# A fused attention and two-mixture kernel: last logits among the next output sums, sums read before low parts, first gathered transposes over two units

## Chip, cores and metric

The kernel runs on one core of a Trainium2 chip. The metric is device microseconds (us) of one execution; a profiled execution also has a span, from its first to its last recorded instruction. Engines are named as in the profile: PE is TensorE (PEld its weight loads), DVE is VectorE, ACT is ScalarE, POOL is GpSimd, SP is SyncE, whose queue issues most DMAs.

## The reference, cut to what matters

Attention with a bucket mask runs first; its output `x` (1536 tokens of 512) goes through a dense layer pair, and the result through a mixture of eight experts, each token by the one expert with the largest logit.

```python
def _moe_ref(x, w_in, w_out, s, b):            # first mixture: 512 -> 2048 -> 512
    h = x @ w_in
    r = np.maximum(h, 0.0)
    g = s * (r * r) + b
    return (g @ w_out).astype(np.float32)

def _moe2_ref(x, modality_id, w_gate, modality_bias, w1, w2):   # second: 8 experts, 512 -> 1024 -> 512
    logits = x @ w_gate + modality_bias[modality_id]
    e_idx = np.argmax(logits, axis=1)
    ...
    for e in range(E):
        mask = e_idx == e
        h = np.maximum(x[mask] @ w1[e], 0.0)
        out[mask] = gate_w[mask, None] * (h @ w2[e])
```

## The kernel before

All products are made from high and low halves: a 32-bit value is split by ACT into a rounded high part and by DVE into the rest, and each product is three matmuls (high x high, high x low, low x high).

**Units.** After attention, PE works through a list of units written out in `program`. The first mixture has three token groups of 512 (`g` = 0, 1, 2) and 16 hidden chunks of 128 (`fc`). A unit `(0, g, fc)` multiplies one hidden chunk into the four output slices `Y0` to `Y3` (`y1`, line 863, 12 matmuls of 512 columns). The last unit of a group ends with `yout` (line 883): DVE adds the saved partial sums `sv` to the four slices and writes the output sums `yt`. The second mixture works on blocks of up to 408 tokens of one expert. A unit `(1, s, fc)` multiplies hidden chunk `fc` (of 8) of block `s` into the same four slices (`sb_o`, line 1181, 12 matmuls of 408 columns). Its last unit ends with `sb_out`, where ACT and DVE copy the slices to `ot` (lines 1191 and 1189).

**Lead.** Each unit first issues the hidden product of the unit two places later (`h1`, line 820, or `sb_h`, line 1161; a product `H` is 12 matmuls). What ACT and DVE do to that product is a post: `r` in the first mixture (lines 826 and 827) and `hh` and `hl` in the second (lines 1168 and 1169), which share their two buffers each with `gh` and `gl` of the first (lines 834 and 835). In the last two units of the first mixture and in all of the second, the post is issued late, after the unit's output sums:

```python
            (self.sb_o if u[0] else self.y1)(u[1], u[2])
            self.flush()
            if late:
                post[0]()
            if u[2] == (7 if u[0] else 15):
                (self.sb_out if u[0] else self.yout)(u[1])
```

**Side jobs.** `at(kind, a, fc, ...)` hangs jobs on a unit. They are taken in their order, one after each quarter of the hidden product if marked with `n > 0` (and as long as the first in the list is so marked), and the rest after the four output slices, as many at a time as makes them fit into four places. The table `MT` says on which `fc` a job stands.

**The jobs around the change.** The tokens of groups 0 and 1 are routed while group 2 is computed. `sb_gather(0)` fetches the rows of block 0 from DRAM with four gathers of POOL (line 1134), of 128, 128, 128 and 24 rows, on unit `(0, 2, 10)`. `sb_xt(0, d)` for `d` = 0 to 3 transposes them, four 128x128 transposes of PE each (`mxt` from `xg`, line 1148), into one of two PSUM banks that all small jobs share in turn; ACT copies the high part `xh` and DVE the low part `xl` (lines 1149 and 1150). All four stand on unit `(0, 2, 13)`, beside the last weight split (lines 1067 and 1068).
On unit `(1, 0, 0)` stand, for the tokens of group 2, four `ylog` (each four matmuls of `yt` by the gate's 8 columns, `ml`, line 891, and an add into the logits `L`, line 893), marked to go between the quarters of the hidden product. Then come `rest_a` (the choice of an expert, lines 917 to 970, and one activation) and two `yrow` (four transposes `mr`, line 900, a copy by ACT, and a store to DRAM by SP's queue, line 904). Unit `(1, 0, 1)` has `rest_b` (rank matmuls, lines 979 to 984, then a chain of DVE up to `pos`, lines 988 to 1026) and six one-hots `M` (line 1088). Unit `(1, 0, 2)` has two more `yrow`, `rest_c` (the expert numbers for SP's loads), the first `sb_pick` (`mid`, line 1100) and six more one-hots.

Of the kernel before, what the change touches and what calls it, by code (L numbers as in the profile page):

```python
# [610 lines left out]
NG = 3  # L611
# [4 lines left out]
class Moe:  # L616
# [618 lines left out]
    def program(self, open_route, end_attn, close_attn, end1):  # L1235
        side = {}
        self.lo_engine = self.nc.vector

        def at(kind, a, fc, *fns, n=0):

            side.setdefault((kind, a, fc), []).extend(([x, None, n > 0], n) for x in fns)

        units = [(0, g, fc) for fs in (range(FA), range(FA, 16)) for g in range(NG) for fc in fs]
        n1 = len(units)
        units += [(1, s, fc) for s in range(NSB) for fc in range(8)]

        def ids(s, n, kind, a, fc, step):
            i = units.index((kind, a, fc))
            for lo in range(0, n, step):
                hi = min(n, lo + step)  # L1250
                at(*units[i], *(lambda tb=tb: self.sb_onehot(s, tb) for tb in range(lo, hi)))
                i += 1
                at(*units[i], lambda lo=lo, hi=hi: self.sb_pick(s, lo, hi), n=(hi - lo) // 2 + 1)
            at(*units[i], lambda: self.sb_ids(s), lambda: self.sb_gather(s))


        at(0, 0, MT["xt"], end_attn)
        at(0, 0, max(MT["xt"], self.led - LEAD), close_attn)
        for i in range(34 - self.wi):
            at(*units[(0, 0, 1, 2)[i] if i < 4 else i * 3 // 4], self.w_next)  # L1260
        for g in range(NG - 1):
            for t in range(4):
                at(0, g + 1, FA + (t + 1, t // 2)[g], lambda g=g, t=t: self.ylog(g, t), n=1)
                at(0, g + 1, FA + t + 1 - g, lambda g=g, t=t: self.yrow(g, t))
        at(0, 1, 14, open_route)
        at(0, 1, 15, lambda: self.setup_route(self.rt))
        g = NG - 1
        at(0, g, MT["fa"], self.first_a)
        at(0, g, MT["fb"], self.first_b)
        at(0, g, MT["fc"], self.first_c)  # L1270
        W0 = self.sb_weights(0, lambda: self.e0[0:1, 0:1])
        for i in range(8):
            at(0, g, MT["w0"] + i // 2, W0[i][0])
            at(0, g, MT["w0"] + (i + 1) // 2 + 1, W0[i][1])
        ids(0, TA, 0, g, MT["i0"], 4)
        for d in range(4):
            at(0, g, MT["x0"], lambda d=d: self.sb_xt(0, d))

        for t in range(4):
            at(1, 0, 0, lambda t=t: self.ylog(NG - 1, t), n=1)  # L1280
        at(1, 0, 0, self.rest_a)
        for t in range(2):
            at(1, 0, MT["ya"], lambda t=t: self.yrow(NG - 1, t))
        at(1, 0, MT["rb"], self.rest_b)
        for t in range(2, 4):
            at(1, 0, MT["yb"], lambda t=t: self.yrow(NG - 1, t))
        at(1, 0, MT["rc"], self.rest_c)
        for s in range(NSB):
            n = s + 1
            if s:  # L1290
                for c in range(NC):
                    at(1, s, c // 2, lambda s=s, c=c: self.sb_store(s - 1, c))
            if n == NSB:
                continue
            ids(n, 12, 1, s - 1 if s else 0, MT["iN"] if s else MT["i1"], MT["sn"] if s else MT["s1"])
            for d in range(4):
                at(1, s, MT["xn"] + d // 2 if s else MT["x1"], lambda n=n, d=d: self.sb_xt(n, d))
            W = self.sb_weights(n, lambda n=n: self.ei[0:1, n:n + 1])
            for i in range(8):
                a = i if s else MT["w1"] + i // 2 + (i == 7)  # L1300
                at(1, s, a, W[i][0])
                if a == 7:
                    at(1, n, 0, W[i][1])
                else:
                    at(1, s, a + 1, W[i][1])

        def lead(u):
            return (self.sb_h if u[0] else self.h1)(u[1], u[2])

        while self.led < LEAD:  # L1310
            self.lead1()
        self.lead2()
        self.lead3(LEAD)
        none = lambda: None
        for i, u in enumerate(units):
            mine = side.pop(u, [])
            self.jobs.extend(x[0] for x in mine)
            if i + LEAD < self.led:
                post = none, self.posts[i + LEAD][0]
            else:  # L1320
                post = lead(units[i + LEAD]) if i + LEAD < len(units) else (none, none)
            late = i + LEAD >= n1
            if not late:
                post[0]()
            self.rate = -(-sum(max(n, 1) for x, n in mine if x in self.jobs) // 4)
            (self.sb_o if u[0] else self.y1)(u[1], u[2])
            self.flush()
            if late:
                post[0]()
            if u[2] == (7 if u[0] else 15):  # L1330
                (self.sb_out if u[0] else self.yout)(u[1])
            elif not u[0] and u[2] == FA - 1:
                self.ysave(u[1])
            if i == n1 - 1:
                end1()
            post[1]()
        for c in range(NC):
            self.sb_store(NSB - 1, c)


LEAD = 2
NST = 3
MT = dict(xt=0, fa=6, fb=7, fc=8, w0=8, i0=8, x0=13, ya=0, yb=2, rb=1, rc=2, i1=1, s1=6, x1=5, xn=3, w1=3, iN=5, sn=6)

FA = 4
NM = 6
# [128 lines left out]
```

## Time and profile before

| what | us |
|---|---|
| median of the three runs shown | 750.51 |
| all three | 757.81, 749.63, 750.51 |
| profiled execution | 752.84 |
| its span | 751.0 |
| PE busy | 698.9 (93%) |
| DVE, ACT, POOL busy | 429.1, 364.7, 248.6 |
| mean granted clock of PE in the profile | 0.966 of full speed |

A timeline row is: start, length, engine, line, operation, what is written from what, shape, count; in brackets the idle time of the engine before it and what ended that. Matmuls overlap, so the step from one start to the next says what one costs. The granted clock is 1.00 at 2.4 GHz and 0.50 at 1.2 GHz.

### The profile page before, as it was taken

What the parts mean: (1) busy time and instruction counts of PE and PEld (TensorE: products, weight loads), DVE (VectorE), ACT (ScalarE), POOL (GpSimd) and SP (SyncE); (2) the same over time, 40 slices, a digit from 0 to 9 for tenths busy, and PEclk for the clock granted to TensorE, in tenths of its full rate; (3) what the DMA queues carried; (4) which work ended last, traced back from release to release, by engine and by line L of the source; (5) the groups of instructions that cost most, each with busy time, mean ns of one, the idle gap of its engine ahead of it and who ended that gap; (6) DMA issues with size and microseconds to landing.
All of it is one profiled execution on the core that took longest, in us unless ns stands there. A gap on an engine that the chain in (4) does not pass through costs nothing.

```text
span 751.0 us, 12828 instructions
## 1 busy us (share of the span) xinstructions
PE 698.9 (93%) x5037; PEld 613.4 (82%) x5037; DVE 429.1 (57%) x781; ACT 364.7 (49%) x562; POOL 248.6 (33%) x251
## 2 busy tenths in 40 slices
PE   6688899999999689999999999999998999999993
PEld 5587788988988677788888888888878989999993
DVE  5455667667667976988773322235653565645311
ACT  2565687877878755655542222222440254434412
POOL 8295777776878860000000000200200024030112
PEclk9699999999999889999999999999997999999998
DMA  6979435645470221534410010002420455435201
GB/s 150 216 173 217 87 72 111 138 108 112 108 183 2 86 85 61 154 123 121 131 57 0 1 43 14 1 29 87 139 72 1 139 160 201 141 109 161 69 17 43
DMA packets 53509, 73.64 MB, mean 98 GB/s; under 512 B 30456, under 2 KB 30968, under 8 KB 53440
## 3 DMA queue, kind: packets, MB, share of 16 engines
q1 hardware_dynamic: 50320, 63.49, 32.3%
q0 software_dynamic: 2960, 9.24, 3.9%
q8 instruction: 41, 0.67, 0.4%
q14 instruction: 28, 0.23, 0.1%
q10 hardware_dynamic: 160, 0.00, 0.0%
HBM read 46.37 MB, written 6.49 MB: 70 GB/s over the span
## 4 chain that ended last, share of the span: by engine, by line
PE 71%; ACT 8%; issue 7%; DVE 6%; POOL 4%; DMA 3%; SPq 0%; POOLq 0%; ACTq 0%; DVEq 0%
PE Y L863 17%; PE H L820 17%; PE H L1161 8%; PE Y L1181 7%; PE Sst L403 5%; PE av L424 5%; ACT e L405 3%; PE Smaxp L357 3%; POOL el L412 2%; PE Sbits L240 2%; PE ml L891 1%; ACT eh L411 1%; DVE v L716 1%; PE Strans L192 1%; PE SH L820 1%
## 5 line engine op out<-in xcount | busy, mean ns | idle before, releaser
L412 POOL TENSOR_TENSOR el<-e,eh 128x768 f16<-128x768 f32 x80 | 133.1, 1668 | 67.8 <-ACT eh L411 55.2
L863 PE MATMUL Y<-gh,W 128*128 128x512 f32 x384 | 131.5, 395 | 0.6 <-DVE sv L873 0.6
L359 DVE TENSOR_REDUCE mx<-Smaxp 128x1 f32<-128x768 f32 x96 | 90.5, 953 | 48.2 <-PE Smaxp L357 48.0
L405 ACT ACTIVATE e<-Sst 128x768 f32<-128x768 f32 x96 | 76.9, 802 | 45.8 <-PE Sst L403 43.5
L403 PE MATMUL Sst<-Q,K 128*128 128x384 f32 x384 | 94.3, 369 | 1.5 <-ACT e L405 1.3
L863 PEld LDWEIGHTS Y<-gh,W 128*128 128x128 f32 x384 | 72.1, 188 | 16.7 <-DVE sv L873 1.1
L1181 PE MATMUL Y<-hh,W 128*128 128x408 f32 x256 | 82.7, 364 | 0.0
L863 PE MATMUL Y<-gl,W 128*128 128x512 f32 x192 | 75.3, 392 | 0.0
L827 DVE SCALAR_TENSOR_TENSOR r<-r,sb 128x512 f32<-128x512 f32 x46 | 35.9, 781 | 68.6 <-ACT r L826 68.6
L403 PEld LDWEIGHTS Sst<-Q,K 128*128 128x128 f32 x384 | 66.3, 198 | 3.7 <-ACT e L405 1.5
L411 ACT ACTIVATE eh<-e 128x768 f16<-128x768 f32 x80 | 67.5, 844 | 2.5
L826 ACT ACTIVATE r<-H 128x512 f32<-128x512 f32 x44 | 26.3, 598 | 81.4 <-PE H L820 81.2
L801 POOL IOTA ev<- 128x96 f32 x1 | 0.3, 299 | 194.3 <-PE H L820 194.3
L357 PE MATMUL Smaxp<-K,Q 96*128 96x384 f32 x192 | 51.6, 359 | 13.3 <-ACT NM L392 4.6
L1134 POOL DMA_INDIRECT xg<-yd,ix x16 | 18.3, 1147 | 129.4 <-DVE nf L1120 69.0
L834 ACT ACTIVATE gh<-r,sb 128x512 fp32r<-128x512 f32 x46 | 33.0, 720 | 51.7 <-PE Y L863 49.8
L835 DVE SCALAR_TENSOR_TENSOR gl<-r,sb,gh 128x512 fp32r<-128x512 f32 x46 | 34.4, 749 | 37.1 <-ACT gh L834 37.1
L424 PE MATMUL av<-VX,eh 128*128 128x65 f16 x960 | 52.6, 197 | 2.0 <-ACT eh L411 2.0
L424 PEld LDWEIGHTS <-eh 128*128 128x128 f16 x960 | 40.2, 100 | 15.0 <-issue 12.1
L357 PEld LDWEIGHTS Smaxp<-K,Q 96*128 96x128 f32 x192 | 35.4, 198 | 18.9 <-ACT NM L392 6.6
L1068 DVE TENSOR_TENSOR W<-st,W 128x1024 fp32r<-128x1024 f32 x32 | 38.9, 1225 | 18.2 <-ACT W L1067 17.8
L1181 PEld LDWEIGHTS Y<-hh,W 128*128 128x128 f32 x256 | 48.9, 192 | 0.0
(321 smaller groups left out, 1485.4 us busy)
## 6 DMA issues: line engine op xcount, KB each, us to landing
st<-in_moe_w_dram SPq DMA_DIRECT2D x32, 512.0 KB
sw<-in_moe_w_in_dram SPq DMA_DIRECT2D x16, 512.0 KB
sw<-in_moe_w_out_dram SPq DMA_DIRECT2D x16, 512.0 KB
Q<-qh SPq DMA_DIRECT2D x32, 192.0 KB
K<-kh SPq DMA_DIRECT2D x32, 192.0 KB
nq<-in_q_dram SPq DMA_DIRECT2D x16, 192.0 KB
nk<-in_k_dram SPq DMA_DIRECT2D x16, 192.0 KB
Q<-ql SPq DMA_DIRECT2D x16, 192.0 KB
```

Source lines behind the costliest of these rows:

```text
L357: nc.tensor.matmul(out=ps[:, a, 0:HALF], lhsT=self.Q1[i][0:96, j * 128:j * 128 + 128], rhs=self.K1[i][0:96, a * HALF:a * HALF + HALF])
L359: nc.vector.tensor_reduce(out=self.mx[h][:, j:j + 1], in_=ps[:, :, 0:HALF], axis=AX.XY, op=ALU.max)
L403: nc.tensor.matmul(out=ps[:, a, 0:HALF], lhsT=K[:, c], rhs=Q[:, a * HALF:a * HALF + HALF], start=(n == 0), stop=(n == 1))
L405: nc.scalar.activation(out=h2(e), in_=ps[:, :, 0:HALF], func=ACTF.Exp, scale=0.125)
L411: nc.scalar.activation(out=eh, in_=e, func=ACTF.Copy)
L412: nc.gpsimd.tensor_tensor(out=el, in0=e, in1=eh, op=ALU.subtract)
L424: mm = lambda q, n, e, v, start=False, stop=False: nc.tensor.matmul(out=av[:, q, 0:n], lhsT=e, rhs=v, start=start, stop=stop, skip_group_c ...
L820: nc.tensor.matmul(out=ps, lhsT=w[:, k, fs], rhs=x[:, k], start=(n == 0), stop=(n == 11))
L863: nc.tensor.matmul(out=self.yp[d], lhsT=w[:, i, ds], rhs=x, start=(fc in (0, FA) and n == 0), stop=(fc in (FA - 1, 15) and n == 2))
L1068: nc.vector.tensor_tensor(out=lo[:, o], in0=d["st"], in1=f(hi[:, o]), op=ALU.subtract)
L1161: nc.tensor.matmul(out=ps, lhsT=w, rhs=xx[:, kd, 0:C], start=(n == 0), stop=(n == 11))
L1181: nc.tensor.matmul(out=self.yp[d][:, 0:C], lhsT=w, rhs=xx, start=(fc == 0 and n == 0), stop=(fc == 7 and n == 2))
```

## The change

Two things are moved; no instruction is added or taken away.

1. The late post is issued after `yout` and `sb_out`. The four `ylog` of the last group are no longer marked to go between the quarters of the hidden product of unit `(1, 0, 0)`: three of them stand after its output slices 0, 1 and 3, the fourth after the first quarter of the hidden product of unit `(1, 0, 1)`. `rest_a` and the first two `yrow` move to that unit's product as well, and four empty jobs keep places ahead of `rest_b`.
2. The transposes of the first gathered rows stand on units `(0, 2, 12)` and `(0, 2, 13)`, two each, with an empty job after each.

```diff
+        nop = lambda: None
...
         for d in range(4):
-            at(0, g, MT["x0"], lambda d=d: self.sb_xt(0, d))
-
-        for t in range(4):
-            at(1, 0, 0, lambda t=t: self.ylog(NG - 1, t), n=1)
-        at(1, 0, 0, self.rest_a)
+            at(0, g, MT["x0"] + d // 2, lambda d=d: self.sb_xt(0, d), nop)
+
+        yl = [lambda t=t: self.ylog(NG - 1, t) for t in range(4)]
+        at(1, 0, 0, yl[0], yl[1], nop, yl[2])
+        at(1, 0, 1, yl[3], self.rest_a, n=1)
         for t in range(2):
-            at(1, 0, MT["ya"], lambda t=t: self.yrow(NG - 1, t))
+            at(1, 0, 1, lambda t=t: self.yrow(NG - 1, t), n=1)
+        at(1, 0, 1, *[nop] * 4)
         at(1, 0, MT["rb"], self.rest_b)
...
             self.flush()
-            if late:
-                post[0]()
             if u[2] == (7 if u[0] else 15):
                 (self.sb_out if u[0] else self.yout)(u[1])
             elif not u[0] and u[2] == FA - 1:
                 self.ysave(u[1])
+            if late:
+                post[0]()
...
-MT = dict(xt=0, fa=6, fb=7, fc=8, w0=8, i0=8, x0=13, ya=0, yb=2, rb=1, rc=2, i1=1, s1=6, x1=5, xn=3, w1=3, iN=5, sn=6)
+MT = dict(xt=0, fa=6, fb=7, fc=8, w0=8, i0=8, x0=12, yb=2, rb=1, rc=2, i1=1, s1=6, x1=5, xn=3, w1=3, iN=5, sn=6)
```

On DVE, at the end of the first mixture, the queue reads as follows before and after (`H_4355` and `H_4356` are the two product banks, `Y_4357` to `Y_4360` the four slices, `mx` is the first step of the choice).

```order
-L1169 SCALAR_TENSOR_TENSOR hl<-H_4356,hh 128x408
 L883 TENSOR_TENSOR yt<-Y_4357,sv_4621 128x512
 L883 TENSOR_TENSOR yt<-Y_4358,sv_4621 128x512
 L883 TENSOR_TENSOR yt<-Y_4359,sv_4621 128x512
 L883 TENSOR_TENSOR yt<-Y_4360,sv_4621 128x512
-L893 TENSOR_TENSOR L<-ml,L 128x8 x4
-L917 TENSOR_REDUCE mx_6609<-L 128x4
-L919 TENSOR_TENSOR eq<-L,mx_6609 128x32
+L1169 SCALAR_TENSOR_TENSOR hl<-H_4356,hh 128x408
+L893 TENSOR_TENSOR L<-ml,L 128x8 x3
+L1169 SCALAR_TENSOR_TENSOR hl<-H_4355,hh 128x408
+L893 TENSOR_TENSOR L<-ml,L 128x8
```

The low part of chunk 1 goes behind the four output sums, and that of chunk 2 behind the first three logits, ahead of the choice.

On PE, at the start of the second mixture, before: the hidden product of chunk 2 with the logits between its quarters.

```order
L1161 MATMUL H_4355<-xh,W 128x408
L1161 MATMUL H_4355<-xl,W 128x408
L1161 MATMUL H_4355<-xh,W 128x408
L891 MATMUL ml<-wg,yt 128x8 x4
L1161 MATMUL H_4355<-xh,W 128x408
L1161 MATMUL H_4355<-xl,W 128x408
L1161 MATMUL H_4355<-xh,W 128x408
L891 MATMUL ml<-wg,yt 128x8 x4
```

The same place after it: the end of that product, and the first two output slices of unit `(1, 0, 0)`.

```order
L1161 MATMUL H_4355<-xl,W 128x408
L1161 MATMUL H_4355<-xh,W 128x408
L1181 MATMUL Y_4357<-hh,W 128x408
L1181 MATMUL Y_4357<-hl,W 128x408
L1181 MATMUL Y_4357<-hh,W 128x408
L891 MATMUL ml<-wg,yt 128x8 x4
L1181 MATMUL Y_4358<-hh,W 128x408
L1181 MATMUL Y_4358<-hl,W 128x408
L1181 MATMUL Y_4358<-hh,W 128x408
L891 MATMUL ml<-wg,yt 128x8 x4
```

The first logits now stand behind the whole product and one output slice.

On PE, in unit `(0, 2, 12)`, between the output slices 1, 2 and 3:

```order
 L863 MATMUL Y_4358<-gl,W 128x512
 L863 MATMUL Y_4358<-gh,W 128x512
+L1148 MATMUL mxt<-ident,xg 128x128 x4
 L863 MATMUL Y_4359<-gh,W 128x512
 L863 MATMUL Y_4359<-gl,W 128x512
 L863 MATMUL Y_4359<-gh,W 128x512
+L1148 MATMUL mxt<-ident,xg 128x128 x4
 L863 MATMUL Y_4360<-gh,W 128x512
 L863 MATMUL Y_4360<-gl,W 128x512
```

Two groups of transposes stand here now, one unit earlier than before.

## Rows read from the trace of the kernel before

**Rows 1.** The page, parts 1 and 2: busy time, and granted clock in 40 slices
```profile
PE 698.9 (93%) x5037; PEld 613.4 (82%) x5037; DVE 429.1 (57%) x781; ACT 364.7 (49%) x562; POOL 248.6 (33%) x251
...
PEclk9699999999999889999999999999997999999998
```

**Rows 2.** Stages of 1 us: busy (x instructions) of PE, PEld, DVE, ACT, POOL; clock, DMA
```profile
572.00:573.00 1.00, 1.00 (x9) 1.00 (x9) 0.17 (x1) 0.00 (x0) 0.00 (x0) 1.00 0.00 0
573.00:574.00 1.00, 1.00 (x6) 1.00 (x6) 0.17 (x1) 0.00 (x0) 0.00 (x0) 0.52 0.06 16
...
583.00:584.00 1.00, 1.00 (x8) 0.93 (x7) 0.00 (x0) 0.19 (x1) 0.00 (x0) 0.86 0.21 84
```

**Rows 3.** Timeline of the seam: start, length, engine, line, what, idle before
```profile
567.84 0.35 PE L1161 MATMUL H<-xh,W 128*128 128x408 f32 x1
568.21 0.34 PE L1161 MATMUL H<-xh,W 128*128 128x408 f32 x1
...
568.58 0.58 DVE L1169 SCALAR_TENSOR_TENSOR hl<-H,hh 128x408 fp32r<-128x408 f32 x1 [4.32 <-ACT hh L1168]
569.08 2.47 DVE L883 TENSOR_TENSOR yt<-Y,sv 128x512 f32<-128x512 f32 x4
...
571.85 0.43 PE L1161 MATMUL H<-xh,W 128*128 128x408 f32 x1
...
579.20 0.17 DVE L893 TENSOR_TENSOR L<-ml,L 128x8 f32<-128x8 f32 x1 [2.56 <-PE ml L891]
...
581.18 0.17 DVE L970 CAST eq<-ohp 128x4 f32<-128x4 bf16 x1
...
586.96 0.26 PE L979 MATMUL mcn<-ohp,oneb 128*128 128x8 bf16 x4
...
588.92 0.35 PE L1161 MATMUL H<-xh,W 128*128 128x408 f32 x1
```

**Rows 4.** Timeline at the first token group's end and its first logits
```profile
418.85 2.47 DVE L883 TENSOR_TENSOR yt<-Y,sv 128x512 f32<-128x512 f32 x4
...
419.80 0.39 PE L863 MATMUL Y<-gh,W 128*128 128x512 f32 x1
...
426.26 0.95 PE L891 MATMUL ml<-wg,yt 128*128 128x8 f32 x8
```

**Rows 5.** The chain in order of time, three pieces at full clock
```profile
556.95 0.44 PE mxt L1148 x4
...
584.34 2.23 PE H L1161 x12
...
599.00 2.22 PE Y L1181 x12
```

**Rows 6.** Timeline: the chain of DVE from the ranks, and PE's first use
```profile
587.36 0.19 DVE L988 TENSOR_TENSOR pf<-mrk,cnt 128x32 f32<-128x32 f32 x1 [1.79 <-PE mrk L984]
...
595.70 1.65 DVE L1088 TENSOR_SCALAR M<-slot,pos 128x512 f16<-128x512 f16 x6
...
596.10 0.52 PE L1100 MATMUL mid<-val,M 128*128 128x6 f16 x8
```

**Rows 7.** Timeline and stage of the transposes of the gathered rows
```profile
555.59 0.66 PE L1148 MATMUL mxt<-ident,xg 128*128 128x128 f32 x4 [1.18 <-DVE xl L1150]
...
550.00:560.00 10.00, 8.82 (x50) 7.49 (x49) 6.74 (x9) 4.76 (x8) 0.53 (x1) 1.00 0.00 1
```

**Rows 8.** Timeline before them, last gather issue, and landing (block 1's, median us)
```profile
543.67 1.08 POOL L1134 DMA_INDIRECT xg<-yd,ix  x1 [0.30 <-issue]
...
547.60 0.62 PE L863 MATMUL Y<-gh,W 128*128 128x512 f32 x2
...
xg<-yd,ix POOLq DMA_INDIRECT x4, 5.6
```

**Rows 9.** Timeline at the end of block 0
```profile
624.41 1.08 ACT L1191 ACTIVATE ot<-Y 128x512 f32<-128x512 f32 x2
...
626.04 0.35 PE L1181 MATMUL Y<-hh,W 128*128 128x408 f32 x1
```

More of the change, by code (lines that the diff above doesn't have):

```diff
@@ L1313, in program @@
         self.lead3(LEAD)
-        none = lambda: None
         for i, u in enumerate(units):
@@ L1318, in program @@
             if i + LEAD < self.led:
-                post = none, self.posts[i + LEAD][0]
+                post = nop, self.posts[i + LEAD][0]
             else:
-                post = lead(units[i + LEAD]) if i + LEAD < len(units) else (none, none)
+                post = lead(units[i + LEAD]) if i + LEAD < len(units) else (nop, nop)
             late = i + LEAD >= n1
```

## The prediction, made before the changed kernel ran

> **What bounds the kernel now.** I read the page first: TensorE (PE) is busy 93% of the span, so a change pays where PE waits or runs at the lower of its two clock levels [rows 1]. In the line of the granted clock the reader finds a 7 in a row of nines about three quarters through: that slice holds the seam between the two mixtures, which is the place of the change. Next I read the seam microsecond by microsecond: the mean granted clock is 1.00 in the microsecond before 573, 0.52 in the one from 573, 0.50 in each of the next nine, and 0.86 in the one from 583 [rows 2]. A mean of 0.52 is 0.96 us at 0.50, one of 0.86 is 0.28 us, so the low level (1.2 GHz instead of 2.4) lasted 0.96 + 9 + 0.28 = 10.2 us. Half of that, 5.1 us, was lost. Then the timeline says what PE did before the clock fell [rows 3]. The product H of block 0, chunk 2 starts at 567.84. Its first three matmuls end at 568.55, and the next H matmul starts only at 571.85. In between stand the first logits (`ml`), which need the output sums `yt`. VectorE (DVE) makes these four from 569.08 on, 2.47 us long, because in its queue they stand behind `hl`, the low part of chunk 1 (568.58). `hl` needs an activation that cannot start before the last output sum of the first mixture is done. So a hole of 3.3 us, with only 0.9 us of logits in it, is followed by ten microseconds at half clock.
>
> **First part: sums ahead of the low part, logits among the next sums.** Moving the call of the delayed post behind `yout` puts the four `yt` ahead of `hl` on DVE. The same sums of the first token group show what they then do: they start at 418.85, while PE is still adding the later output slices (its last of that unit starts at 419.80) [rows 4]. Each takes 0.62 and starts when its slice is done: for the last group the last slice ends about 568.0, so the last `yt` ends near 568.7. The first logits now come after the whole of chunk 2's product and three output sums, 2.24 + 0.55 us behind the start, at 570.6 on the old time axis. That leaves 1.9 us of cover, so this wait goes to zero. `hl` of chunk 1 then ends about 569.35 instead of 569.16; it is first read a unit later, 4 us off, and costs nothing.
>
> What PE has to do from the start of that product (567.84) to the start of chunk 4's product (588.92 [rows 3]) at full clock is the following. Two products of 2.23 us make 4.46, two sets of output sums of 2.22 make 4.44 [rows 5]. Two groups of four transposes at 0.44, that is 0.11 for one [rows 5], make 0.88. Four groups of logits are eight such instructions each, 0.88 at 0.11 (the row of a group in the first mixture has 0.95 with its overlap into the next [rows 4]); that makes 3.52. The rank matmuls take 0.26 [rows 3]. Sum: 13.56 us. Before, the same stretch took 588.92 - 567.84 = 21.08. The difference is 7.5 us: 5.1 of clock and 2.4 of waiting.
>
> What is late next: the rank matmuls now stand behind two output slices of chunk 1 instead of one, because the jobs ahead of them fill the first slice (three places each). That is 0.55 us later against PE's own work. Behind them DVE runs one chain without a hole, from the ranks at 587.36 to the second six one-hots, which start at 595.70 and take 0.28 each. PE's first group on these, at 596.10, takes the first two of them, and the second is ready only at 596.25 [rows 6]: PE is at the chain's heels already. So those 0.55 us come back as a wait of PE there. Bounds: 0 (if DVE finds slack) and 0.6. I take 0.5, since I see no gap in the chain. The ranks themselves need the four rest logits chosen: DVE's choice took 2.2 us from the adding of the last logit at 579.20 to 581.35 [rows 3], and PE has three quarters of a product (1.7), two groups of transposes (0.9) and two output slices (1.1) between, 3.7 us; no wait. The row transposes move from the first unit to the second; their ScalarE copies and their two stores on the SP queue keep their place before the expert numbers are read there, so weights and gather of the second block start from the same DVE chain as before and move with PE.
>
> **Second part: transposes of the first gathered rows over two units.** Before, all four groups stand in one unit; the third waited 1.18 us for DVE to free its PSUM bank, and the clock stayed at 1.00 through it [rows 7]. Now two groups stand in the unit before, behind its sixth output sum. The sixth starts at 547.60, one more 0.23 later, so the first group begins at 547.83 [rows 8], and six sums and a whole product lie between the second and the third group. The bank wait goes: -1.2. But the first group moves up by nearly a unit towards the gather that fills it. POOL starts the last of the four gather issues at 543.67; the one landing time that the trace has for such gathers is 5.6 us [rows 8]. That puts the rows at 549.27, while PE wants the last quarter at about 548.2: a wait of 1.1. So this part is worth between -1.2 (rows there in time) and -0.1; I take -0.4, near to the row. The copies behind these two groups, on ScalarE and DVE, have a whole product's time before PE wants their banks again, and nothing else of PE needs them so early.
>
> The Trainium skill (DMA: Bandwidth & Descriptors, Anatomy of one DMA) gives a transfer about 2.0 us of fixed cost, most of it the wait until the last byte is confirmed. By that, an estimate from its figure, the last gather, whose issue ends at 544.75, would be in place before 547.83 and the part would be worth the full 1.2; the trace's 5.6 us speaks against it and is what I use.
>
> **Third part: the posts behind `sb_out`.** The same move puts ScalarE's and DVE's copies of a block's sums ahead of `hh`/`hl` at three block ends. There the copies start at 624.41, after `hh`, and PE writes the first of these banks again at 626.04 without waiting [rows 9]. They become earlier, `hh` later by about half a microsecond, and PE reads it 4 us after. Zero; bounds -0.2 and +0.2.
>
> **Sum.** -7.5 + 0.5 - 0.4 = -7.4 us. The profiled execution took 752.84 (span 751.0 and 1.84 around it), so it would take 745.4. It is 2.3 us above the median of the runs shown, 750.51; against that the sum gives 743.1. How long the clock stays low may differ from execution to execution, and a run 2.3 us shorter may have had less of it: then 5.1 us are left. I weigh this with a fifth and take 7.0: 743.5 us.
>
> **Rivals.**
> 1. The clock falls all the same. The logits now stand in a row of short groups of 8-column matmuls between output sums, and if PE looks idle enough there, the 5.1 us stay lost: saving 2.3, 748.2 us. For it: in the old seam the clock came back only when groups of logits were over. Against it: there a 3.3 us hole preceded; in the new order each group of 0.88 has 0.55 or more of dense matmuls on both sides, and behind the 1.18 us wait with its transposes the clock held [rows 7]. Chance 0.08.
> 2. PE runs into something that has not moved: the second block's weights or gather. These transfers start from the DVE chain, which moves with PE, but if the stores and loads between take the same wall time from an older point, half of the gain is given back: saving 3.7, 746.8 us. Chance 0.10.
> 3. Slower. The new first transposes wait for the gather, the clock falls at about 551 and stays down through the seam, where transposes and logits keep PE thin. Low clock costs half of its length; the sum turns to a loss when it lasts longer than 2 x 7.4 = 14.8 us. With 20 us it is 10 lost against 7.4 saved: 753.1 us. Against it: the wait is 1.1 us at most by the row, as long as the 1.18 after which the clock held. Chance 0.03.
> That the change doesn't do what it says is not among them: the order of instructions shows both moves.
>
> **How the numbers follow.** Forecast 0.79, rivals 0.08, 0.10, 0.03. The forecast's own range is 741.0 (8.7 saved, and 0.9 between the two lower runs shown) to 746.0 (the 5.1 case with the whole gather wait). The range takes in the first two rivals: 740.8 to 748.2. A measurement of this kernel tells about 1% from no change, which is 743.0 here, just below the forecast: faster by over 1% gets 0.40, within 1% 0.58 (the rest of the forecast, both saving rivals, most of the third), slower by over 1% 0.02.
>
> **What would show it.** Right: `yt` rows that start before the last output sums end, no PE wait at the first `ml`, a granted clock of 1.00 through the seam, and about 13.6 to 14.1 us from the product of chunk 2 to that of chunk 4. The first transposes of `xg` wait at most 1.1 us and the third none. A wait of about half a microsecond before the second six `mid`. Wrong: a stretch at 0.50 after the logits, a wait of several microseconds at the first `xg` transposes, or a seam as computed with a total that shrinks by less than 5 us, which would mean that the time is met again later, in the second block.

## The result and the profile after

The changed kernel takes 745.63 us (median of 14 runs, 739.87 to 748.74). The kernel before, run beside it 14 times, takes 753.87 us. The ratio is 0.9882, with a 95% interval of 0.9859 to 0.9905: by it 8.9 us are saved, between 7.2 and 10.6 (the two medians lie 8.2 apart). The forecast was 743.5 us, 7.0 saved. A second comparison further down gives 0.9844 (0.9817 to 0.9870).

The profiled execution of the changed kernel took 741.36 us, its span is 739.6. On the page, the 7 that stood three quarters through the clock line [rows 1] is a 9 now, and PE is busy for 11.2 us less with the same 5037 matmuls:

```profile
PE 687.7 (93%) x5037; PEld 603.6 (82%) x5037; DVE 428.9 (58%) x781; ACT 365.0 (49%) x562; POOL 247.8 (34%) x251
...
PEclk9899999999999899999999999999999999999997
```

Stages of 1 us, of the seam after (columns as in [rows 2]): the granted clock, the third number from the end, is 1.00 in every one of the fourteen from 562 to 576; three of them stand here.

```profile
562.00:563.00 1.00, 1.00 (x6) 0.81 (x5) 1.00 (x2) 0.00 (x0) 0.00 (x0) 1.00 0.00 0
...
572.00:573.00 1.00, 1.00 (x10) 0.95 (x8) 0.86 (x6) 0.20 (x1) 0.00 (x0) 1.00 0.00 0
573.00:574.00 1.00, 1.00 (x11) 0.96 (x8) 0.66 (x4) 0.63 (x2) 0.00 (x0) 1.00 0.00 0
```

The timeline of the seam after, against [rows 3]:

```profile
561.10 2.73 DVE L883 TENSOR_TENSOR yt<-Y,sv 128x512 f32<-128x512 f32 x4 [1.73 <-PE Y L863]
...
562.71 0.39 PE L863 MATMUL Y<-gh,W 128*128 128x512 f32 x1
562.94 0.35 PE L1161 MATMUL H<-xh,W 128*128 128x408 f32 x1
...
563.75 0.57 DVE L1169 SCALAR_TENSOR_TENSOR hl<-H,hh 128x408 fp32r<-128x408 f32 x1
...
565.73 0.95 PE L891 MATMUL ml<-wg,yt 128*128 128x8 f32 x8
...
570.62 0.95 PE L891 MATMUL ml<-wg,yt 128*128 128x8 f32 x8
...
573.60 0.17 DVE L970 CAST eq<-ohp 128x4 f32<-128x4 bf16 x1
...
575.19 0.25 PE L979 MATMUL mcn<-ohp,oneb 128*128 128x8 bf16 x4
...
576.60 0.35 PE L1161 MATMUL H<-xh,W 128*128 128x408 f32 x1
```

The reader sees three things. `yt` starts at 561.10, while PE still adds output slices (the last sum of the first mixture starts at 562.71), and `hl` follows it. The first logits at 565.73 stand behind the whole product without a bracket: no wait. And from the product of chunk 2 (562.94) to that of chunk 4 (576.60) it takes 13.66 us; before, 21.08.

The new wait, in the timeline behind the ranks, against [rows 6] (0.42 in the bracket; by the steps from start to start PE loses 0.54 here):

```profile
583.92 1.66 DVE L1088 TENSOR_SCALAR M<-slot,pos 128x512 f16<-128x512 f16 x6
...
584.32 0.52 PE L1100 MATMUL mid<-val,M 128*128 128x6 f16 x8 [0.42 <-DVE M L1088]
```

The transposes of the gathered rows, against [rows 7] and [rows 8]; first the last gather's issue:

```profile
539.50 1.07 POOL L1134 DMA_INDIRECT xg<-yd,ix  x1 [0.30 <-issue]
...
543.65 0.49 PE L1148 MATMUL mxt<-ident,xg 128*128 128x128 f32 x3
...
544.59 0.30 PE L1148 MATMUL mxt<-ident,xg 128*128 128x128 f32 x1 [0.45 <-DMA xg<-yd,ix]
...
550.06 0.60 PE L1148 MATMUL mxt<-ident,xg 128*128 128x128 f32 x4
```

The third group, which had waited 1.18 us, waits for nothing; the fourth transpose of the first group waits 0.45 us for the last gather, and starts 544.59 - 539.50 = 5.1 us after that gather's issue began.

**What of the 11.4 us between the two spans (751.0 and 739.6) is the change.** The seam gives 21.08 - 13.66 = 7.42. The transposes give 1.18 - 0.45 = 0.73. Ahead of all that, the output sums of unit `(0, 2, 12)` start 4.2 us earlier than before (542.27 against 546.44), where no instruction has moved. From the product of chunk 4 to the end it takes 0.9 us more (163.0 against 162.1), with the new wait in it; in the second profile of the changed kernel (experiment 12), with the same wait, that stretch takes 739.5 - 577.45 = 162.0, so the rest of the 0.9 is spread from execution to execution. The 4.2 us arise before the first token group's `yt`, which stood at 418.85 [rows 4]:

```profile
414.68 2.47 DVE L883 TENSOR_TENSOR yt<-Y,sv 128x512 f32<-128x512 f32 x4
```

They go with the granted clock in the attention stage. Two of its stretches, before:

```profile
60.00:90.00 30.00, 25.71 (x275) 22.27 (x275) 17.68 (x29) 20.12 (x32) 19.11 (x19) 0.89 0.66 141
240.00:300.00 60.00, 50.14 (x443) 42.36 (x442) 47.84 (x57) 37.01 (x59) 33.27 (x21) 0.89 0.24 71
```

and after:

```profile
60.00:90.00 30.00, 24.17 (x282) 20.71 (x282) 19.20 (x34) 21.44 (x33) 20.04 (x19) 1.00 0.70 152
240.00:300.00 60.00, 50.07 (x437) 42.19 (x437) 50.88 (x63) 39.04 (x62) 31.99 (x21) 0.94 0.28 85
```

Granted clocks of 0.89 became 1.00 and 0.94. The stretch from 60 to 90 shows 1.00 in two later profiles of other kernels here and 0.83 in three, and experiments 3 and 7, one and the same kernel, reach their seams at 568.05 and 563.72. So this is a spread from execution to execution, and one profile set beside one other carries several microseconds of it; that the clock makes up all of the 4.2 is not shown. The experiments are therefore read in two ways: the ratio to the kernel before, timed on the same chip, and the length and waits of the seam in the trace.

### The profile page after: what moved, and what is told of

It reads as the page before. It is cut to its first block, busy times and chain, and to the rows that moved or that the text cites. A ratio compares the mean times of both kernels' runs of the same rounds, so it can differ in the third digit from the quotient of the medians.

```text
span 739.6 us, 12831 instructions
## 1 busy us (share of the span) xinstructions
PE 687.7 (93%) x5037; PEld 603.6 (82%) x5037; DVE 428.9 (58%) x781; ACT 365.0 (49%) x562; POOL 247.8 (34%) x251
## 4 chain that ended last, share of the span: by engine, by line
PE 68%; ACT 7%; issue 7%; DVE 6%; POOL 4%; DMA 4%; SPq 2%; POOLq 0%; ACTq 0%; DVEq 0%
PE Y L863 17%; PE H L820 16%; PE H L1161 8%; PE Y L1181 7%; PE av L424 5%; PE Sst L403 5%; ACT e L405 3%; PE Smaxp L357 3%; PE Sbits L240 2%; POOL el L412 2%; ACT eh L411 1%; DVE v L716 1%; PE ml L891 1%; DMA K<-aux 1%; PE Strans L192 1%
## 5 line engine op out<-in xcount | busy, mean ns | idle before, releaser
L403 PE MATMUL Sst<-Q,K 128*128 128x384 f32 x384 | 92.6, 364 | 1.4 <-ACT e L405 1.2
```

The lines of the kernel that those rows point to most:

```text
L403: nc.tensor.matmul(out=ps[:, a, 0:HALF], lhsT=K[:, c], rhs=Q[:, a * HALF:a * HALF + HALF], start=(n == 0), stop=(n == 1))
```

## Experiments

The seam is timed in each trace as above, from the start of chunk 2's product to that of chunk 4's. The medians of the kernel before beside these runs are 753.92 (experiments 1 to 4), 753.62 (5 to 8), 754.08 (9 and 10) and 755.00 (11 and 12).

**1. The seam alone.** The changed kernel, with the transposes all on one unit as before.

```diff
-            at(0, g, MT["x0"] + d // 2, lambda d=d: self.sb_xt(0, d), nop)
+            at(0, g, 13, lambda d=d: self.sb_xt(0, d))
```

> The change without its second part: the four groups of transposes of the first gathered rows stand on one unit again. Theory (the gain is the seam: 2.4 us of waiting and about 5 us of low clock): from the product of chunk 2 to that of chunk 4 it takes 13.6 to 13.8 us as in the changed kernel, the clock is 1.00 there, the third group of transposes waits about 1.2 us again, and the time falls by 7 to 7.5 us, ratio 0.990. Rival (the spread of the transposes is what keeps the clock up): the clock falls behind the logits again and the time falls by 3 us or less, ratio 0.996 or more.

Measured: 744.99 us, ratio 0.9891 (0.9835 to 0.9946). The seam is 582.37 - 568.71 = 13.66 us, at a clock of 1.00. The wait at the transposes is back:

```profile
556.46 0.65 PE L1148 MATMUL mxt<-ident,xg 128*128 128x128 f32 x4 [1.19 <-DVE xl L1150]
```

So the seam carries nearly all of the gain.

**2. The transposes alone.** The kernel before, with only these spread.

```diff
-            at(0, g, MT["x0"], lambda d=d: self.sb_xt(0, d))
+            at(0, g, 12 + d // 2, lambda d=d: self.sb_xt(0, d), lambda: None)
```

> The kernel before with the second part alone: transposes of the first gathered rows on two units. Theory: the first group waits 0.4 to 0.5 us for the gather, the third no longer waits 1.2 us, the hole before the logits (3.3 us) and the 10 us at clock 0.50 stay; the time falls by 0.7 us, ratio 0.999. Rival (the wait of the transposes prepares the fall of the clock): the clock stays at 1.00 through the seam, and the time falls by 5 us or more, ratio 0.993.

Measured: 752.30 us, ratio 0.9976 (0.9957 to 0.9995), 1.8 us less with an interval from 0.4 to 3.2; the trace accounts for 1.18 - 0.20 = 1.0. The hole of the seam stays:

```profile
548.82 0.30 PE L1148 MATMUL mxt<-ident,xg 128*128 128x128 f32 x1 [0.20 <-DMA xg<-yd,ix]
...
569.24 2.30 PE L891 MATMUL ml<-wg,yt 128*128 128x8 f32 x8 [1.35 <-DVE yt L883]
```

and behind it the clock falls, now for longer than in [rows 2]:

```profile
569.00:570.00 1.00, 0.61 (x4) 0.55 (x4) 1.00 (x3) 0.00 (x0) 0.00 (x0) 0.94 0.00 0
570.00:571.00 1.00, 0.90 (x5) 0.71 (x4) 0.89 (x2) 0.00 (x0) 0.00 (x0) 0.50 0.00 0
...
583.00:584.00 1.00, 1.00 (x8) 0.91 (x6) 0.00 (x0) 0.44 (x1) 0.00 (x0) 0.73 0.00 0
```

It is 0.50 in every stage from 570 to 583; with 0.12 us of the stage before and 0.54 of the one behind, 13.7 us at the low level, where the profile of the kernel before shows 10.2. The seam took 589.35 - 567.17 = 22.18 us instead of 21.08. The order is the same in both; how long the clock stays down is not. What differs most is the fall: here it comes 2.8 us behind the start of chunk 2's product, still inside the hole, and there 5.2 us behind it. The clock comes back in nearly the same place, at the second group of row transposes (`mr`): at 583.54 with the group at 583.59 here, at 583.28 with the group at 583.07 there.

**3 and 7. Sums first, logits where they were.** The kernel before, with only `yout` put ahead of the late post.

```diff
+            if u[2] == 15 and not u[0]:
+                self.yout(u[1])
             if late:
                 post[0]()
-            if u[2] == (7 if u[0] else 15):
-                (self.sb_out if u[0] else self.yout)(u[1])
+            if u[2] == 7 and u[0]:
+                self.sb_out(u[1])
```

> The kernel before with one edit: the output sums of the last group are issued ahead of the late post; the logits stay between the quarters of the product of chunk 2. Theory (the hole alone brings the clock down): the last sum ends 0.2 us after the product's first quarter, the first logits wait 0.2 to 0.5 us, the clock stays at 1.00, and the time falls by 6.5 to 7.3 us, ratio 0.991. Rival (the logits themselves are too thin: four groups of 0.9 us with 0.56 us of product between them): the clock falls to 0.50 again behind them, and only 2 to 3 us are saved, ratio 0.997.

Measured: 747.49 us, ratio 0.9919 (0.9881 to 0.9958). The expected wait of 0.2 to 0.5 us didn't come. The logits, between the quarters of the product again, find their sums ready:

```profile
566.21 2.73 DVE L883 TENSOR_TENSOR yt<-Y,sv 128x512 f32<-128x512 f32 x4 [1.73 <-PE Y L863]
...
568.61 0.95 PE L891 MATMUL ml<-wg,yt 128*128 128x8 f32 x8
```

The seam is 581.72 - 568.05 = 13.67 us, clock 1.00. As the ranks stand no later than before in this order, the wait of 0.42 isn't there. The same kernel in a second execution (experiment 7):

> A second look at the kernel with the output sums ahead of the late post and the logits between quarters of the product (as e3). If only waiting brings the clock down, it is at 1.00 through the seam again. If logits between quarters are thin enough to do it in some executions, as the filled hole suggests (low for 3.8 us there with no wait), this execution may show the clock at 0.50 for 3 to 7 us behind the second to fourth logits.

Measured: 741.36 us in one run, seam 577.39 - 563.72 = 13.67 us, clock 1.00, no wait at any of the four groups of logits. (The low stretch of the filled hole, experiment 4, measures 3.4 us, not 3.8.)

**5. Logits later, post still ahead of the sums.** The changed kernel with the old order of the post, and transposes on one unit.

```diff
-            at(0, g, MT["x0"] + d // 2, lambda d=d: self.sb_xt(0, d), nop)
+            at(0, g, 13, lambda d=d: self.sb_xt(0, d))
...
+            if late:
+                post[0]()
             if u[2] == (7 if u[0] else 15):
                 (self.sb_out if u[0] else self.yout)(u[1])
             elif not u[0] and u[2] == FA - 1:
                 self.ysave(u[1])
-            if late:
-                post[0]()
```

> The other half of the seam alone: logits among the output sums of the next units as in the changed kernel, but the late post stays ahead of the output sums, and the transposes stay on one unit. Theory (each of the two edits by itself takes most of the hole): the last sum ends 3.8 us behind the start of the product of chunk 2, so the first logits wait about 1.0 us behind one output slice; the clock stays at 1.00; the time falls by 6 to 6.5 us, ratio 0.992. Rival (only the order on the vector engine counts): the hole and the low clock stay, ratio 0.998 or more.

Measured: 745.90 us, ratio 0.9885 (0.9844 to 0.9926).

```profile
565.61 2.47 DVE L883 TENSOR_TENSOR yt<-Y,sv 128x512 f32<-128x512 f32 x4
...
567.17 0.77 PE L891 MATMUL ml<-wg,yt 128*128 128x8 f32 x6
...
568.14 0.39 PE L891 MATMUL ml<-wg,yt 128*128 128x8 f32 x2 [0.21 <-DVE yt L883]
```

The wait that was expected came out at 0.21 us. The group waits for each slice's sum, not for all four: six of its eight matmuls ran while DVE made the last sum (565.61 + 2.47 = 568.08). The clock stayed at 1.00, and the seam is 578.45 - 564.37 = 14.08 us. So either of the two edits alone takes away the hole; together they gain little more than one.

**4. The hole filled with unread matmuls.** The kernel before, with 14 additional matmuls of 408 columns ahead of the first logits; nobody reads what they write.

```diff
-        pl = self.m("ml")
+        pl = self.fill(g, t) or self.m("ml")
...
+        for i in range(14):
+            self.nc.tensor.matmul(out=ps[:, 0:C], lhsT=w[:, 0:128], rhs=x[:, 0, 0:C], start=True, stop=True)
```

> The kernel before with fourteen matmuls of 408 columns, whose result nobody reads, ahead of the first logits. They take 2.6 us of the hole in which the tensor engine waits for the sums. Theory (the idle hole brings the clock down): the product goes on at the same time as before, 3.3 us after its first quarter or up to 0.5 later, but the clock stays at 1.00, and the time falls by 4.5 to 5 us, ratio 0.994. Rival (the thin logits behind the hole bring it down): clock 0.50 as before, and the time is the same, ratio 1.000.

Measured: 751.59 us, ratio 0.9965 (0.9937 to 0.9992), 2.6 us saved, between the two expectations. In the trace the seam is 584.88 - 566.99 = 17.89 us: about the 13.66 of the changed kernel, 2.6 for the filling and 1.7 of clock. Through the filled hole the clock is 1.00, and the logits behind it wait for nothing:

```profile
567.55 2.73 PE L1440 MATMUL mfill<-xh,W 128*128 128x408 f32 x14
570.12 1.03 PE L891 MATMUL ml<-wg,yt 128*128 128x8 f32 x8
```

But it falls five microseconds later, behind the last of the logits between the quarters, without a wait of PE in the seam:

```profile
575.00:576.00 1.00, 1.00 (x8) 0.99 (x8) 0.39 (x3) 0.00 (x0) 0.00 (x0) 0.81 0.00 0
576.00:577.00 1.00, 1.00 (x5) 0.97 (x4) 0.90 (x6) 0.23 (x1) 0.00 (x0) 0.50 0.00 0
...
579.00:580.00 1.00, 1.00 (x9) 0.95 (x8) 0.00 (x0) 0.25 (x2) 0.00 (x0) 0.98 0.11 43
```

That is 0.38 + 3 + 0.04 = 3.4 us at 0.50, 1.7 us lost. So with the hole filled the clock held where it had fallen, and a hole isn't the only thing that can bring it down. Experiments 3 and 7 have the same order of logits without the hole, and there the clock held in both profiles; why it fell in this one stays open.

**6. The four groups of logits in one row.** The changed kernel, with all 32 logit matmuls behind output slice 0.

```diff
-        at(1, 0, 0, yl[0], yl[1], nop, yl[2])
-        at(1, 0, 1, yl[3], self.rest_a, n=1)
+        at(1, 0, 0, lambda: [x() for x in yl][0], nop, nop, nop)
+        at(1, 0, 1, self.rest_a, n=1)
```

> The changed kernel with the four groups of logits one behind the other after the first output slice, 3.5 us of nothing but matmuls of 8 columns, and no wait of the tensor engine. Theory A (only waiting brings the clock down): clock 1.00, the time of the changed kernel, ratio 0.988 to 0.990. Theory B (matmuls of 8 columns count little, so a row of them is like a hole): the clock is at 0.50 for 3 us or more behind the row although the engine never waits, 1.7 to 3.4 us are lost, ratio 0.992 to 0.994.

Measured: 748.00 us, ratio 0.9907 (0.9873 to 0.9942). The ratio lies between the two theories and does not decide; the trace does, for B:

```profile
569.73 3.63 PE L891 MATMUL ml<-wg,yt 128*128 128x8 f32 x32
```

```profile
572.00:573.00 1.00, 1.00 (x12) 1.00 (x11) 0.17 (x1) 0.00 (x0) 0.00 (x0) 1.00 0.00 0
573.00:574.00 1.00, 1.00 (x7) 0.99 (x7) 0.17 (x1) 0.00 (x0) 0.00 (x0) 0.66 0.00 0
...
576.00:577.00 1.00, 1.00 (x5) 0.99 (x4) 0.00 (x0) 0.44 (x1) 0.00 (x0) 0.63 0.00 0
```

The row waits for nothing, and PE and its weight loads are busy throughout. Still the clock falls to 0.50 behind it (0.50 in the two stages that are left out; 3.4 us in all), and the seam is 582.18 - 566.93 = 15.25 us, 1.6 longer than with the logits spread. The mechanism of the prediction's rival 1 exists. In the changed kernel an output slice, or a quarter of a product, of full matmuls stands between the groups, and the clock held in all eight profiles with that order (the changed kernel, experiments 1, 5 and 8 to 12).

**8. The posts ahead of `sb_out` again.** The changed kernel, with the prediction's third part undone.

```diff
-            if u[2] == (7 if u[0] else 15):
-                (self.sb_out if u[0] else self.yout)(u[1])
+            if u[2] == 15 and not u[0]:
+                self.yout(u[1])
+            if late:
+                post[0]()
+            if u[2] == 7 and u[0]:
+                self.sb_out(u[1])
             elif not u[0] and u[2] == FA - 1:
                 self.ysave(u[1])
-            if late:
-                post[0]()
```

> The changed kernel with the copies of a block's sums behind the late post again at the three block ends, as before the change; the output sums of the first mixture stay ahead. Theory (these moves are worth nothing): no wait of the tensor engine of over 0.1 us at the three block ends in this kernel or in the changed one, and the same time within the spread. Rival: waits of 0.2 to 0.5 us at the block ends that the changed kernel does not have.

Measured: 744.35 us in one run. PE's waits in the second mixture are those of the changed kernel: 0.30 at the first `mid` (as in the kernel before), 0.42 at the second one-hots, 0.78 and 0.22 later (0.78 and 0.23 there), none at the ends of the first three blocks. The part is worth nothing that these traces show. In two profiles with the posts behind `sb_out` PE waited for `hl` once, 0.45 us at 633 in experiment 6 and 0.27 at 630 in experiment 9. Both stand three units behind the end of block 0, where the posts have the same order in both kernels, and in both DVE reached that `hl` late, behind a weight split; nothing in them ties the wait to the move.

**9. The ranks one slice earlier.** The changed kernel without its four empty jobs.

```diff
-        at(1, 0, 1, *[nop] * 4)
```

> The changed kernel without its four empty jobs, so the rank matmuls stand one output slice (0.55 us) earlier in the second unit of the second mixture. Theory (the 0.42 us wait at the second six one-hots is the price of the ranks' later place): that wait shrinks to 0.2 or less, unless something else holds the ranks. Rival (the wait has to do with DVE's chain alone and not with the place of the ranks): it stays at 0.4. A gain here may come back as a wait of the rank matmuls themselves for ACT's copy of the rows before them, up to 0.3 us. The time as a whole moves by less than 0.5 us, which one run does not tell.

Measured: 743.09 us in one run. The wait of 0.42 is gone. In its place the ranks wait for ScalarE's copy of the row before them:

```profile
576.63 0.60 ACT L903 ACTIVATE row<-mr 128x512 f32<-128x512 f32 x1 [0.40 <-PE mr L900]
...
576.81 0.35 PE L1181 MATMUL Y<-hh,W 128*128 128x408 f32 x1
577.28 0.24 PE L979 MATMUL mcn<-ohp,oneb 128*128 128x8 bf16 x4
...
577.48 0.44 PE L1181 MATMUL Y<-hh,W 128*128 128x408 f32 x1
```

The copy ends at 576.63 + 0.60 = 577.23, and the ranks start at 577.28. From the last output sum ahead of the ranks to the first behind them it takes 0.67 us, where the changed kernel has 575.40 - 575.00 = 0.40. The seam grows by 0.28, to 579.24 - 565.30 = 13.94. No bracket shows this wait; it is seen only in the step from one start to the next. What the empty jobs bring and what they cost nearly cancel.

**10. The first transposes one output slice later.**

```diff
-            at(0, g, MT["x0"] + d // 2, lambda d=d: self.sb_xt(0, d), nop)
+            at(0, g, MT["x0"] + d // 2, *([nop] * 2 if d == 0 else []), lambda d=d: self.sb_xt(0, d), nop)
```

> The changed kernel with the first two groups of transposes of the gathered rows one output slice (0.7 us) later in their unit. Theory (the 0.45 us wait of the last of the first four transposes is for the landing of the last gather, 5.1 us after its issue starts): the wait is 0, and the third group still has none; the kernel gains 0.45 us, less than the timing tells (same within 0.5%). Rival (the wait is for the order of the jobs, so PE waits wherever the group stands): 0.4 or more remains.

Measured: 743.73 us, ratio 0.9866 (0.9825 to 0.9908). No transposes wait. This alone doesn't show that the later place did it, as experiments 11 and 12 tell.

**11 and 12. Both waits out, and the changed kernel beside it.** Experiment 11 has the edits of 9 and 10 together; 12 is the changed kernel once more.

> Both edits of the two runs before together: the first transposes one output slice later, and no empty jobs ahead of the ranks. Theory (the two waits are separate, each in its own place): neither the 0.45 us wait for the gather nor the 0.42 us wait at the second six one-hots is there, and the kernel is 0.9 us shorter than the changed kernel at the same mean granted clock; the timing of this kernel, which spreads by some 4 us either way, tells it as the same as the changed kernel. Rival: one of them comes back in another place between the second transposes and the second block.

> The changed kernel unchanged, beside the version before it on the same chip. Theory: a seam of 13.66 us at clock 1.00, the two waits of 0.45 and 0.42, and a median 0 to 1.5 us above the version without these waits; what is left of the spread goes with the mean granted clock, lost in the attention stage. Rival (the seam's clock of 1.00 was chance): a stretch at 0.50 behind the logits between the output slices in this profile.

Measured: 745.12 us, ratio 0.9876 (0.9853 to 0.9900) without the two waits, and 742.21 us, ratio 0.9844 (0.9817 to 0.9870) for the changed kernel. In the trace of 11:

```profile
544.91 1.08 POOL L1134 DMA_INDIRECT xg<-yd,ix  x1 [0.30 <-issue]
...
550.56 0.30 PE L1148 MATMUL mxt<-ident,xg 128*128 128x128 f32 x1 [0.33 <-DMA xg<-yd,ix]
```

and in that of 12:

```profile
540.74 1.07 POOL L1134 DMA_INDIRECT xg<-yd,ix  x1 [0.30 <-issue]
...
544.89 0.86 PE L1148 MATMUL mxt<-ident,xg 128*128 128x128 f32 x4
...
545.50 0.48 PE L863 MATMUL Y<-gh,W 128*128 128x512 f32 x1
...
563.79 0.35 PE L1161 MATMUL H<-xh,W 128*128 128x408 f32 x1
...
577.45 0.35 PE L1161 MATMUL H<-xh,W 128*128 128x408 f32 x1
...
585.18 0.52 PE L1100 MATMUL mid<-val,M 128*128 128x6 f16 x8 [0.42 <-DVE M L1088]
```

The wait for the gather does not sit in the order alone. In 12, the first transposes start 544.89 - 540.74 = 4.15 us behind the last issue, as in the first profile of the changed kernel (543.65 - 539.50), and no bracket marks a wait. But the row of four is 0.86 us long where one without a wait is 0.60, and the next output sum starts 0.61 us behind it instead of 0.36: the fourth transpose came about 0.25 late, at 545.45, 4.7 us after the issue. In the first profile the same step is 1.00, so 0.64 were lost there, more than its bracket of 0.45. In 11 the transposes start 0.7 us later after the issue and the fourth still waits: there it started 550.56 - 544.91 = 5.65 us after the issue. The expectations of 0 (in 11) and of 0.45 (in 12) both missed. The seam of 12 is 13.66 us with the clock at 1.00 once more; that of 11 is 582.14 - 568.22 = 13.92, with the ranks' 0.28. Experiment 11 did not beat the changed kernel: its median is 2.9 us above that of 12, where 0 to 1.5 below was expected. Its profiled span is 4.0 us longer (743.5 against 739.5), and it reaches the seam 568.22 - 563.79 = 4.4 us later; its clock in the attention stage is lower, 0.83 from 60 to 90 against 0.89 and 0.89 from 240 to 300 against 0.94. Whether 11 gains anything stays open: its six executions alone spread from 744.02 to 748.17.

## Why the prediction was right, and where it was off

**The hole and the clock behind it.** As predicted: `yt` ahead of `hl`, no wait at the first logits, 1.00 through the seam, 13.66 us where 13.56 were summed. Experiments 3 and 5 show the hole to be the cause, each removing it in another way, with ratios of 0.9919 and 0.9885 and seams at full clock: the clock fell in both profiles with the hole (the kernel before, experiment 2) and held in ten without it; the two others without it are experiments 4 and 6. Experiment 4 separates its two costs: with PE kept busy in the hole, the clock held there, and fell only behind the fourth group of logits. "Either edit would do" was not in the prediction, which treated the two as one.

**The new wait behind the ranks.** Predicted 0.5, measured 0.42 in the bracket and 0.54 by the steps, for the named reason: in experiments 3 and 9, with the ranks earlier, it is not there. What the prediction did not see is why the empty jobs are there at all: without them the ranks wait 0.28 for a copy by ScalarE.

**The transposes.** The bank wait of 1.18 went, as said. The new wait for the gather was put at up to 1.1 from one landing time of 5.6 us, and near 0.8 was taken. Six profiles with the transposes in this place show 0.45 (the changed kernel), 0.20 (experiments 2 and 9) and no wait that is marked (6, 8 and 12; by the steps 0.11, 0.06 and 0.25). The wait was put too high, by the brackets by 0.35 us against the first of these and by more against the others, since one landing time was taken for a constant; the trace of the changed kernel lists landings of such gathers from 3.4 to 6.4 us. The Trainium skill's fixed cost of about 2.0 us (DMA: Bandwidth & Descriptors, Anatomy of one DMA) would have had no wait at all; the landing 5.1 us after the issue's start in the changed kernel's own profile speaks against it here, and the measurement decides.

**The posts behind `sb_out`.** Zero, as predicted, as far as the traces of experiment 8 and the changed kernel show.

**The rivals.** Rival 1 did not happen in the changed order, but its mechanism is shown by experiments 4 and 6: behind thin logits the clock fell with PE never waiting. It cost 1.7 us there, not the 5.1 that the rival was priced at. Rival 2 is out: behind the seam the trace is 0.9 us longer than before in one profile and no longer in the other (experiment 12), not 3.7. Rival 3 is out with a gather wait of 0.45 us (0.64 by the steps) and the clock at 1.00 behind it.

**From the sum to the time: the step that failed.** The sum against the profiled execution was 7.4 us; the traces give 7.42 + 0.73 - 0.42 = 7.7. The prediction then went down to 7.0, on the guess that a run near the median had had less low clock than the profiled one. Nothing bears that guess out: in the only other profile with the same hole (experiment 2) the clock stayed low for 13.7 us, not 10.2, and the measured saving is 8.9 (7.2 to 10.6). One such profile doesn't show how long the low clock lasts in most executions; how the 1.2 us between 7.7 and 8.9 come about stays open. And the level was taken from three runs with a median of 750.51, where 14 give 753.87. The two errors partly cancel, which is luck: 743.5 against 745.63. The chances suffered more: "within 1%" was the likelier, and the ratio came out at 0.9882, with an interval that only just reaches 1%.

## What to carry to other kernels

Price a wait of TensorE together with the granted clock in the stages behind it: here 2.4 us of waiting cost 5.1 us more in clock, and one reordering of DVE's queue recovered both. Before moving a consumer later, look whether its producer merely stands behind something in its own queue; either repair was enough here. And before a difference of a few microseconds between two profiles is explained, compare when they reach the place of the change: 4.2 of the 11.4 us here had nothing to do with it.

## What was not expected of the hardware

A row of 32 logit matmuls of 8 columns, 3.63 us without any wait and with PE busy by every row, was followed by a granted clock of 0.50 and 1.6 us more of seam (experiment 6); a share of busy time of 1.00 does not tell that the clock will hold. Around the same hole the clock stayed at 0.50 for 10.2 us in one profile and 13.7 in another, mostly because it fell 2.4 us earlier. And the transpose that needs the same gather of 24 rows could start 5.1 us after the start of its issue in one execution, 5.65 in another and 4.7 in a third.
